# Second-stage units made whole in every chunk of a fused long convolution and gated network on one core

## The chip, the cores and the metric

The kernel runs on one core of one Trainium2 chip. The time is device microseconds from launch to end on that core. The profile names the engines PE (matrix products), PEld (loads of the stationary operand, beside PE), DVE (vector), ACT (scalar functions), POOL (general purpose) and SP, which here only issues transfers. All data are float32; each matrix product of the program shows as two records in the trace, and so does each load of its stationary operand.

## The reference, cut to what matters

```python
x = q = A_q[0]                        # 2048 x 512
g = sigmoid((x * gate_w).sum(-1, keepdims=True))
# branch a
ks = sum(shift(k, ks_ - 1 - j) * shift_k[:, j] for j in range(4))   # causal, 4 taps
kv = ks * v
y = irfft(rfft(kv, 2 * S) * rfft(ssm_k, 2 * S))[:S] + kv * ssm_D    # along the sequence
a = q * y
# branch b
r = x @ w_r
idx = the 2 tokens with the largest r
xs = x[idx]
upd = ((silu(xs @ w_gate) * (xs @ w_up)) @ w_down) * sigmoid(r[idx])
b = x with upd added at rows idx
out = g * a + (1 - g) * b
```

## The kernel before

The 512 channels are worked off in four chunks c of 128. The long convolution is a Fourier transform in two stages written as matrix products, a product in the frequency domain, and two stages back. The steps of a chunk, with the names that stand in the program's order:

- P taps: the four-tap filter as 32x32 matrix products with diagonal matrices, into PSUM; X untap: a DVE transpose of the result into the tile ks; V values: ks times v into the tile kv, on POOL. Chunk 0 does P, X and V in two halves (0a, 0b) over the sequence; chunks 1 to 3 do P and X in one piece.
- A and C: the first stage for the filter and for kv, four batches b each; E and H: the DVE transposes of their results into the tile e. D adds the skip weight into the filter's data, on POOL.
- U: a unit of the second stage into two PSUM banks; G: an ACT copy of one of its two factors (of both, where POOL multiplies); M: the product of the factors into the tile y, on DVE, or on POOL for the units in POOL_PROD. Chunks 1 and 2 have eight whole units w (128 channels each, 16 products of 256 columns). Chunks 0 and 3 (HALF) have eight half units: 64 channels, 32 products of 128 columns, so that I of one half needs four of the eight.
- Q: two POOL passes that sum products in y, so that I needs fewer matrix products; I: the third stage, one for each half hf of the channels, into four banks; F: its transpose on DVE into one of three slots of f; J: the fourth stage, O and K: gate, residual and q; S: the store. In chunk 3 the sums Q are made for half 0 only.

The second branch runs between these: R.0 to R.7 (router and gate), R.cp, R.rr (a transfer into row form), R.mx, R.ix (the two largest, DVE), R.ti, R.xs (gather), then G.g0 to G.u7 (gate and up projections, 16 weight tiles through a ring of four slots wff), G.d0 to G.d7 (down projection, the same ring), G.cp, G.sel, G.upd, and the scatters Z. For the last chunk the residual part goes to a DRAM tile q1 (SQ), Zs adds the update there, and Lq1 brings it back for K.

All of it is recorded in the order of one text, ORDER, which names each step, and behind an @ the PSUM bank or ring slot that it takes. Each engine runs its own steps in that order, and SP issues the loads (Lk, Lh, Lv, Lq, Ls and so on) in it; a step waits for what it reads and for the slot that it writes.

Of the kernel before, what the change touches and what calls it, by code (L numbers as in the profile page):

```python
# [43 lines left out]
M.0.5 Q.0.6 Q.0.4 I.0.0@0 Lk.2@0 X.1 D.2 Q.0.5 F.0.0 R.0@4 R.1 Ls.4@0 R.2 Ls.5@1 D.3 R.3 V.1.1 Ls.6@2 A.1.0@6 Ls.7@3
V.1.2 A.1.2@0 E.1.0 A.1.3@2 V.1.0 E.1.2 C.1.1@6 Lh.4@1 Lv.5@2 V.1.3 A.1.1@0 E.1.3 R.4 Lh.5@0 E.1.1 Lv.6@0 C.1.0@2
Ls.8@0 H.1.1 C.1.2@0 R.5 H.1.0 R.6 Ls.9@1 C.1.3@6 Ls.10@2 H.1.2 R.7 D.4 H.1.3 I.0.1@0 Ls.11@3 R.cp R.rr R.T@5 F.0.1
D.5 U.1.4@6 R.gate U.1.5@4 G.1.4@0 U.1.0@0 M.1.4 G.1.5@1 U.1.1@2 G.1.0@0 M.1.5 U.1.6@6 M.1.0 G.1.1@1 Q.1.2 U.1.7@4
G.1.6@0 M.1.1 J.0.1@0 G.1.7@0 J.0.2@1 O.0.1@0 M.1.7 M.1.6 J.0.0@6 R.mx O.0.2@1 J.0.3@7 U.1.2@4 K.0.1 R.ix P.2@0
G.1.2@1 K.0.2 S.0.1 O.0.0@0 Q.1.0 S.0.2 O.0.3@1 M.1.2 R.ti Lq.1.2@1 U.1.3@4 Lk.3@0 X.2 Lq.1.3@2 K.0.0 A.2.1@6 G.1.3@0
R.xs S.0.0 A.2.3@4 E.2.1 V.2.3 A.2.0@0 E.2.3 A.2.2@2 Lh.6@1 V.2.0 C.2.3@6 E.2.0 Lh.7@0 V.2.2 R.xT@4 Lq.2.0@0 E.2.2  # L50
C.2.0@0 R.xc Lv.7@2 K.0.3 C.2.2@4 H.2.3 G.g0@2 Q.1.3 S.0.3 G.g1 H.2.2 Ls.12@0 G.g2 Ls.13@1 G.g3 R.rs@3 Ls.14@2 H.2.0
P.3@4 Ls.15@3 R.sg D.7 R.fac V.2.1 R.oi Lq.2.1@3 M.1.3 C.2.1@0 X.3 G.g4 D.6 G.g5 Q.1.1 Ls.16@0 G.g6 Ls.17@1 G.g7 H.2.1
Ls.18@2 A.3.3@4 G.sig Ls.19@3 G.m0 A.3.0@6 V.3.3 E.3.3 I.1.1@0 V.3.2 E.3.0 A.3.1@4 V.3.0 F.1.1 A.3.2@6 V.3.1 E.3.1
# [5 lines left out]
C.3.1@0 G.d4 H.3.2 GQ0.1 Lq.3.2@2 G.d5 SQ.0 Q.2.0 C.3.0@6 H.3.1 GQ1.1@1 G.d6 H.3.0 G.d7 GQ0.2 Lq.3.3@1 I.2.0@0 SQ.1
G.cp U.3.0@6 GQ1.2@0 F.2.0 U.3.2@4 G.3.0@0 SQ.2 G.3.2@1 M.3.0 I.2.1@0 GQ1.3@1 M.3.2 Q.3.0 GQ0.3 SQ.3 G.sel@6 F.2.1  # L60
U.3.3@4 Q.3.2 G.upd U.3.1@6 G.3.3@0 M.3.3 U.3.7@0 Z.0 G.3.1@1 U.3.5@2 M.3.1 G.3.7@0 Q.3.3 J.2.0@4 G.3.5@1 M.3.7
U.3.4@6 Q.3.1 O.2.0@0 M.3.5 J.2.3@5 G.3.4@0 K.2.0 I.3.0@0 O.2.3@1 M.3.4 Zs S.2.0 U.3.6@6 F.3.0 K.2.3 J.2.1@4 G.3.6@1
Z.1 S.2.3 J.2.2@5 O.2.1@0 M.3.6 Lq1 J.3.00@0 O.2.2@1 J.3.01@1 K.2.1 O.3.01@0 S.2.1 I.3.1@4 K.2.2 O.3.00@1 S.2.2 K.3.01
# [5 lines left out]
def mixed_kernel(ctx: ExitStack, tc: tile.TileContext, a: dict):  # L69
# [71 lines left out]
    add("Lk.0a", load_k, 0, 0)  # L141
    add("Lk.0b", load_k, 0, 1)
    for c in range(1, NC):
        add(f"Lk.{c}", load_k, c)
# [570 lines left out]
```

## Time and profile before

| | |
|---|---|
| median of three runs | 184.55 us (183.42 to 187.08) |
| profiled execution: time, and span of its instructions | 182.8 us, 181.0 us |
| PE busy | 150.8 us, 3,234 matrix-product records |
| PEld, DVE, POOL, ACT busy | 84.2, 114.5, 94.1, 52.5 us |
| mean granted PE clock | 0.929 |
| moved by DMA | 41.62 MB, 230 GB/s over the span |

The profile is of one execution: the first two lines differ by 1.8 us inside that execution (launch and end), and the median of the runs lies 1.75 us above it. Busy time counts an engine's instructions, so that the span less an engine's busy time is what it stood idle. Lines L... are those of the kernel before.

### The profile page before, as it was taken

To read this page: it belongs to the slowest core of one execution; us is meant where nothing else is said; L and a number is where in the kernel's file an instruction comes from. 1 tells how busy PE (TensorE), PEld (TensorE's weight loads), DVE (VectorE), ACT (ScalarE), POOL (GpSimd) and SP (SyncE) were. 2 spreads that over 40 slices of the span, in tenths; PEclk is the share of its full clock that TensorE was granted. 3 is DMA by queue.
4 is the path that set the end of the run, shared out by engine and by line. 5 is a ranking of instruction groups with operands and counts; after the bars stand their busy time and mean duration, and the time that the engine had idled before them with its cause. 6 is when DMAs were issued, how large, how long until landed. Compare 5 with 4: busy or idle time off the path is not lost.

```text
span 181.0 us, 7115 instructions
## 1 busy us (share of the span) xinstructions
PE 150.8 (83%) x3234; PEld 84.2 (47%) x3234; DVE 114.5 (63%) x90; ACT 52.5 (29%) x123; POOL 94.1 (52%) x94
## 2 busy tenths in 40 slices
PE   7939993497999999999896899999927979799840
PEld 7825353383343366743451234575402346559340
DVE  1025895546489879969799679512970388736462
ACT  3000020222000136851000100499217757467000
POOL 0033406539191006998985820699980026676841
PEclk9996996569999999999999699999985899999997
DMA  5999999900299990068899901999589711016623
GB/s 156 367 380 405 409 412 415 363 21 7 43 352 408 414 369 12 32 173 336 282 364 359 325 30 20 376 252 278 172 263 321 243 66 62 4 62 192 231 106 116
DMA packets 14143, 41.62 MB, mean 230 GB/s; under 512 B 2007, under 2 KB 2336, under 8 KB 13474
## 3 DMA queue, kind: packets, MB, share of 16 engines
q1 hardware_dynamic: 13954, 41.17, 63.9%
q8 instruction: 25, 0.41, 1.0%
q0 software_dynamic: 160, 0.01, 0.1%
q14 instruction: 4, 0.03, 0.0%
HBM read 35.91 MB, written 5.25 MB: 227 GB/s over the span
## 4 chain that ended last, share of the span: by engine, by line
PE 52%; POOL 11%; issue 11%; DMA 10%; DVE 9%; ACT 3%; SPq 1%; POOLq 0%; DVEq 0%
PE ps L287 11%; PE ps L251 8%; PE ps L341 8%; PE ps L244 7%; DMA wff<-in_wg_dram 4%; PE ps L364 4%; DVE f L344 4%; DMA pe<-in_qrow_dram,ti 3%; PE ps L174 3%; POOL y L325 3%; PE ps L194 3%; POOL qN L381 3%; DMA wff<-in_wd_dram 3%; POOL y L326 3%; PE ps L587 2%
## 5 line engine op out<-in xcount | busy, mean ns | idle before, releaser
L237 DVE STREAM_TRANSPOSE e<-ps 128x1024 f32<-128x1024 f32 x32 | 37.9, 1224 | 11.1 <-PE ps L251 8.1
L287 PE MATMUL ps<-e,w 64*32 64x128 f32 (+1 forms) x1536 | 37.7, 330 | 8.5 <-issue 8.5
L314 DVE TENSOR_TENSOR y<-ps,g 128x1024 f32<-128x1024 f32 x28 | 33.3, 1220 | 17.3 <-ACT g L299 17.0
L325 POOL TENSOR_TENSOR y<-y 128x256 f32<-128x256 f32 (+1 forms) x20 | 19.0, 952 | 34.2 <-DVE y L314 34.1
L287 PEld LDWEIGHTS ps<-e,w 64*32 64x32 f32 x1536 | 26.8, 113 | 20.5 <-issue 15.8
L299 ACT ACTIVATE g<-ps 128x512 f32<-128x512 f32 x28 | 16.7, 601 | 48.8 <-PE ps L287 45.9
L215 POOL TENSOR_TENSOR kv<-ks,vN 128x512 f32<-128x512 f32 x16 | 19.9, 1273 | 13.3 <-DVE ks L205 5.8
L344 DVE STREAM_TRANSPOSE f<-ps 128x2048 f32<-128x2048 f32 x8 | 18.5, 2314 | 7.4 <-PE ps L341 7.4
L194 PE MATMUL ps<-kT,diag 32*32 32x512 f32 (+1 forms) x640 | 19.6, 512 | 4.1 <-issue 4.1
L341 PE MATMUL ps<-y,c 32*64 32x512 f32 x288 | 18.7, 615 | 0.5 <-DVE f L344 0.5
L326 POOL TENSOR_TENSOR y<-y 128x256 f32<-128x256 f32 (+1 forms) x20 | 19.0, 951 | 0.0
L244 PE MATMUL ps<-hN,c 64*128 64x512 f32 x64 | 18.8, 721 | 0.2 <-issue 0.2
L377 ACT ACTIVATE o<-ps,omg,gcol 128x128 f32<-128x128 f32 x48 | 17.5, 468 | 3.2 <-PE ps L364 3.2
L364 PE MATMUL ps<-f,vv 128*64 128x128 f32 (+1 forms) x320 | 15.9, 252 | 2.4 <-DVE f L344 2.4
L381 POOL TENSOR_TENSOR qN<-o,qN 128x512 f32<-128x512 f32 x12 | 15.5, 1296 | 4.3 <-ACT o L377 4.0
L251 PE MATMUL ps<-kv,c 64*128 64x512 f32 x64 | 17.4, 655 | 0.0
L364 PEld LDWEIGHTS ps<-f,vv 128*64 128x64 f32 x320 | 14.4, 135 | 5.1 <-DVE f L344 3.4
L194 PEld LDWEIGHTS ps<-kT,diag 32*32 32x32 f32 x640 | 9.9, 103 | 11.3 <-issue 8.5
L314 POOL TENSOR_TENSOR y<-g 128x1024 f32<-128x1024 f32 x4 | 9.6, 2403 | 9.5 <-ACT g L296 9.5
L244 PEld LDWEIGHTS ps<-hN,c 64*128 64x128 f32 x64 | 6.9, 221 | 10.1 <-issue 8.1
L234 POOL TENSOR_TENSOR hN<-hN,drow 65x32 f32<-65x32 f32 x8 | 2.1, 266 | 16.9 <-DMA hN<-in_hN_dram 15.8
L341 PEld LDWEIGHTS ps<-y,c 32*64 32x64 f32 x288 | 6.1, 129 | 9.9 <-issue 7.7
(59 smaller groups left out, 103.9 us busy)
## 6 DMA issues: line engine op xcount, KB each, us to landing
hN<-in_hN_dram SPq DMA_DIRECT2D x8, 512.0 KB, 6.0
vN<-in_vN_dram SPq DMA_DIRECT2D x8, 512.0 KB, 7.1
qN<-in_qN_dram SPq DMA_DIRECT2D x16, 256.0 KB, 6.0
wff<-in_qT_dram SPq DMA_DIRECT2D x8, 512.0 KB, 7.0
wff<-in_wg_dram SPq DMA_DIRECT2D x8, 448.0 KB, 6.7
wff<-in_wu_dram SPq DMA_DIRECT2D x8, 448.0 KB, 4.9
wff<-in_wd_dram SPq DMA_DIRECT2D x8, 448.0 KB, 5.9
kT<-in_kT_dram SPq DMA_DIRECT2D x3, 1120.0 KB, 5.9
```

Source lines behind the costliest of these rows:

```text
L194: nc.tensor.matmul(p[32 * g:32 * g + 32, i, 0:32 * nm], diag[r, 4 * c + j], x, start=(j == 0), stop=(j == 3), skip_group_check=True)
L237: nc.vector.transpose(e[:, place[c, i], b * 16:b * 16 + 16].rearrange("p d k e -> p d e k"), p)
L244: nc.tensor.matmul(p[:, j], w1[r], x[r, 16 * (b % 2):16 * (b % 2) + 16], start=True, stop=True)
L251: nc.tensor.matmul(p[:, par].rearrange("p (d e m) -> p d e m", e=2, m=16), w1[r], x[r], start=True, stop=True)
L287: nc.tensor.matmul(po[32 * j:32 * j + 32, b, ri, :, u], w2[r, k, j, 32 * ri:32 * ri + 32], xs[r, :, :, 8 * j + k, :], start=(ri == 0 and u ...
L314: eng.tensor_mul(z, x.unsqueeze(3).broadcast_to(n).rearrange("p b k h d -> p (b k) h d"), g.unsqueeze(2).broadcast_to(n).rearrange("p b k ...
L325: nc.gpsimd.tensor_tensor(z[:, :, 0, 0], z[:, :, 0, 0], z[:, :, 1, 1], op=ALU.subtract)
L326: nc.gpsimd.tensor_tensor(z[:, :, 0, 1], z[:, :, 0, 1], z[:, :, 1, 0], op=ALU.add)
L341: nc.tensor.matmul(o, w3[r, w], x, start=(n == 0), stop=(n == len(parts) - 1), skip_group_check=True)
L344: nc.vector.transpose(f[:, (2 * c + hf) % 3].rearrange("p d n e -> p d e n"), P["I", c, hf].rearrange("p j (d u) -> p d j u", u=8))
L364: nc.tensor.matmul(p[64 * par:64 * par + 64, i], vv[:, k], x[..., k, :], start=(i == 0), stop=True, skip_group_check=True)
L381: (nc.vector if (c, m) in KDVE else nc.gpsimd).tensor_mul(qn, tiles["o", (c, m)], qn)
```

## The change

Six things are done together:

- Chunks 0 and 3 get whole units, as chunks 1 and 2 have; U, G, M and Q lose their half forms.
- Chunk 0's taps are one run of 64 products of 512 columns behind one load of k; the result goes to two pairs of banks that the order places, and X is two DVE transposes, one for each pair, in every chunk. ks and kv are fixed tiles; gq and q1u (the gate's and the residual's tiles of the last chunk) lie in them. v is laid out on the host so that V reads both operands in a row.
- The sums Q are of whole pairs; in chunk 3 two of the four pairs are summed, and I multiplies the other two unsummed: 16 products of 512 and 16 of 256 columns for each half, where before it were 16 of 512 for half 0 and 32 of 512 for half 1.
- POOL multiplies units 0 and 3 of chunk 0 too (and unit 5 in place of 6 of chunk 2); V.2.0 and V.3.0 move to DVE.
- The start: 4 warm-up products of 512 columns instead of 16 of 128; the step W (an early sigmoid) stands behind the router's gate, so that ACT loads a second function table there.
- ORDER is written anew. `staged` is never called, since STAGE is empty.

```diff
-HALF, LAST = (0, 3), 3
+LAST = 3
-WARM = 16
+WARM = 4
-POOL_PROD = {(1, 3), (1, 6), (2, 3), (2, 6)}
+POOL_PROD = {(0, 0), (0, 3), (1, 3), (1, 6), (2, 3), (2, 5)}
+VDVE = {(2, 0), (3, 0)}
+STAGE = set()
-...(2, 0), (2, 1), (2, 2), (2, 3), (3, 0, 0), (3, 0, 1), (3, 0, 2), (3, 0, 3)}
+...(2, 0), (2, 1), (2, 2), (2, 3), (3, 0), (3, 1)}
 ORDER = """
...
+PW Lc Lk.0@0 Lh.0@0 Ldr Lh.1@1 Lv.0@0 Ls.0@0 DG Lv.1@1 Ls.1@1 Lw2a Ls.2@2 Lc2 Lv.2@2 Lq.0.0@0 P.0@0,2 D.0 D.1 A.0.3@4
...
+    ks = const.tile([128, 4, 512], F32, name="ks")
+    kv = const.tile([128, DC // 2, 16, 2], F32, name="kv")
+    gq = ks.rearrange("p i (m d) -> p (i m) d", d=HC).rearrange("p (h m) d -> p h m d", h=2)
+    q1u = kv.rearrange("p d m e -> p (d m e)").rearrange("p (m d) -> p m d", d=DC)
...
-        z = const.tile([128, 128], F32, name="zero")
+        z = const.tile([128, 512], F32, name="zero")
...
-            nc.tensor.matmul(ps[:, 7, 0:128], z, z, start=True, stop=True)
+            nc.tensor.matmul(ps[:, 7], z[:, 0:128], z, start=True, stop=True)
...
+    def taps(c):
         kt = tiles["kT", c]
+        p = P["P", c] = [ps[:, x:x + 2] for x in at]
         for j in range(4):
             for i in range(4):
                 r = slice(32 * i, 32 * i + 32)
+                x = kt[r, 64 * (3 - j):64 * (3 - j) + 2048].rearrange("p (m z) -> p m z", z=128)
                 for g in range(4):
+                    nc.tensor.matmul(p[i // 2][32 * g:32 * g + 32, i % 2], diag[r, 4 * c + j], x[:, :, 32 * g:32 * g + 32],
                                      start=(j == 0), stop=(j == 3), skip_group_check=True)
...
+    def untap(c, h):
+        nc.vector.transpose(ks[:, 2 * h:2 * h + 2], P["P", c][h])
+
+    def values(c, b):
+        v = tiles["vN", 2 * c + b // 2].rearrange("p (i n) -> p i n", i=2)
+        (nc.vector if (c, b) in VDVE else nc.gpsimd).tensor_mul(
+            kv[:, 16 * b:16 * b + 16].rearrange("p d m e -> p m d e"),
+            ks[:, b].rearrange("p (m d e) -> p m d e", d=16, e=2),
+            v[:, b % 2].rearrange("p (m d e) -> p m d e", d=16, e=2))
...
     def U(c, w):
...
-        if half:
-            xs = xs[:, :, d0 // 2:d0 // 2 + 32]
         pb = P["U", c, w] = bank(2)
+        po = pb.rearrange("p b (r i d) -> p b r i d", r=2, i=2)
+        for ri in range(2):
+            for j in range(4):
+                for b in range(2):
+                    r = slice(64 * b, 64 * b + 64)
+                    nc.tensor.matmul(po[32 * j:32 * j + 32, b, ri], w2[r, w, j, 32 * ri:32 * ri + 32],
+                                     xs[r, :, :, 8 * j + w, :], start=(ri == 0), stop=True, skip_group_check=True)
...
+    def Q(c, v):
+        z = y[:, v].rearrange("p b k h d u -> p b k h (d u)")
```

What the order shows of it, at three places. On PE, from the warm-up to the end of chunk 0's units (`zero` is the warm-up, `kT,diag` P, `hN` A, `kv` C, `e,w` U, `wff,c` R, `y,c` I), before:

```order
L174 MATMUL ps<-zero 128x128 x16
L194 MATMUL ps<-kT,diag 32x256 x128
L244 MATMUL ps<-hN,c_75 128x512 x8
L251 MATMUL ps<-kv,c_75 128x512 x8
L287 MATMUL ps<-e,w_78 32x2x64 x256
L194 MATMUL ps<-kT,diag 32x512 x64
L341 MATMUL ps<-y,c_76 64x512 x16
```

and now:

```order
L174 MATMUL ps<-zero 128x512 x4
L190 MATMUL ps<-kT,diag 32x512 x64
L229 MATMUL ps<-hN,c_75 128x512 x6
L236 MATMUL ps<-kv,c_75 128x512 x2
L229 MATMUL ps<-hN,c_75 128x512 x2
L236 MATMUL ps<-kv,c_75 128x512 x6
L229 MATMUL ps<-hN,c_75 128x512 x4
L264 MATMUL ps<-e,w_78 32x256 x128
L229 MATMUL ps<-hN,c_75 128x512 x2
L415 MATMUL ps<-wff,c_76 32x256 x8
L190 MATMUL ps<-kT,diag 32x512 x64
```

P.0 and the units have half as many products, two batches A of chunk 1 stand ahead of the units, A.2.0 and the first R ahead of P.1, and I.0.0 has gone from behind P.1 to a later place. On DVE in the same stretch (`ks` X, `e` E and H, `y` M, `f` F), before:

```order
L205 STREAM_TRANSPOSE ks<-ps 128x4x8x32 x2
L237 STREAM_TRANSPOSE e<-ps 128x16x2x32 x7
L314 TENSOR_TENSOR y<-ps,g 128x8x2x64 x2
L237 STREAM_TRANSPOSE e<-ps 128x16x2x32
L314 TENSOR_TENSOR y<-ps,g 128x8x2x64 x6
L203 STREAM_TRANSPOSE ks<-ps 128x4x16x32
```

and now:

```order
L194 STREAM_TRANSPOSE ks<-ps 128x1024 x2
L218 STREAM_TRANSPOSE e<-ps 128x16x2x32 x10
L285 TENSOR_TENSOR y<-ps,g 128x1024 x6
L218 STREAM_TRANSPOSE e<-ps 128x16x2x32
L194 STREAM_TRANSPOSE ks<-ps 128x1024 x2
```

All eight exchanges of chunk 0 and two of chunk 1 now stand ahead of the products M, of which two have gone to POOL. On PE at the end (`f,vv` J, `y,c` I, `pe,c` G.sel), before:

```order
L287 MATMUL ps<-e,w_78 32x2x64 x128
L364 MATMUL ps<-f,vv 64x128 x8
L287 MATMUL ps<-e,w_78 32x2x64 x32
L364 MATMUL ps<-f,vv 64x128 x8
L341 MATMUL ps<-y,c_76 64x512 x16
L287 MATMUL ps<-e,w_78 32x2x64 x32
L364 MATMUL ps<-f,vv 64x128 x16
L364 MATMUL ps<-f,vv 64x64 x32
L341 MATMUL ps<-y,c_76 64x512 x32
L364 MATMUL ps<-f,vv 64x64 x32
```

and now (`wff,hT` is G.d):

```order
L264 MATMUL ps<-e,w_78 32x256 x32
L553 MATMUL ps<-wff,hT 32x256 x16
L333 MATMUL ps<-f,vv 64x128 x16
L568 MATMUL ps<-pe_1620,c_76 2x512
L310 MATMUL ps<-y,c_76 64x512 x16
L310 MATMUL ps<-y,c_76 64x64x4 x16
L310 MATMUL ps<-y,c_76 64x512 x16
L310 MATMUL ps<-y,c_76 64x64x4 x16
L333 MATMUL ps<-f,vv 64x64 x64
```

The first I of the last chunk stood ahead of its last unit; now both stand behind all units, behind the down projection and behind G.sel. The four steps O of the last chunk stand on DVE behind both F, two of which stood ahead of the last F before; O.3.01 and O.3.11 take the slots of the ring o that O.3.00 and O.3.10 took.

## Rows read from the trace of the kernel before

**Rows 1.** Page, part 1: busy time, share of the span, records.
```profile
PE 150.8 (83%) x3234; PEld 84.2 (47%) x3234; DVE 114.5 (63%) x90; ACT 52.5 (29%) x123; POOL 94.1 (52%) x94
```
**Rows 2.** PE in order of time: start, us, what, count [idle before it].
```profile
6.70 4.00 PE L194 MATMUL ps<-kT,diag 32*32 32x256 f32 x191
13.65 1.50 PE L194 MATMUL ps<-kT,diag 32*32 32x256 f32 x65 [2.95 <-issue]
...
23.99 2.80 PE L287 MATMUL ps<-e,w 64*32 64x128 f32 x155
29.93 3.66 PE L287 MATMUL ps<-e,w 64*32 64x128 f32 x128 [3.15 <-issue]
35.98 3.48 PE L287 MATMUL ps<-e,w 64*32 64x128 f32 x128 [2.39 <-issue]
...
43.63 4.02 PE L194 MATMUL ps<-kT,diag 32*32 32x512 f32 x102 [1.13 <-issue]
```
**Rows 3.** DMA queues of the page: packets, MB, share.
```profile
q8 instruction: 25, 0.41, 1.0%
```
**Rows 4.** Stretches: length, busy (records) by engine, granted PE clock, DMA share, GB/s.
```profile
29.93:33.60 3.67, 3.66 (x128) 3.21 (x127) 1.23 (x1) 1.01 (x2) 0.30 (x2) 0.50 1.02 414
39.71:42.50 2.79, 2.79 (x127) 1.68 (x128) 2.49 (x3) 1.32 (x3) 2.52 (x4) 1.00 0.02 6
81.15:175.94 94.79, 81.05 (x1650) 42.29 (x1650) 61.85 (x48) 35.10 (x87) 58.27 (x50) 0.95 0.63 208
```
**Rows 5.** Who waited for whom, PE: us in total, times, longest.
```profile
PE ps L587 <- DMA wff<-in_wd_dram: 4.4, 2, 4.0
```
**Rows 6.** PE in order of time, 50 to 80 us: R, A, I, U, J, P.
```profile
50.12 1.93 PE L449 MATMUL ps<-wff,c 128*32 128x256 f32 x32 [0.49 <-DVE ks L203]
51.99 2.85 PE L244 MATMUL ps<-hN,c 64*128 64x512 f32 x12
...
61.88 2.07 PE L341 MATMUL ps<-y,c 32*64 32x512 f32 x32
...
65.06 5.96 PE L287 MATMUL ps<-e,w 64*32 64x256 f32 x192
70.95 3.75 PE L364 MATMUL ps<-f,vv 128*64 128x128 f32 x64
...
75.65 4.46 PE L194 MATMUL ps<-kT,diag 32*32 32x512 f32 x128
```
**Rows 7.** Groups by line and shape: busy us, mean ns | idle before.
```profile
L237 DVE STREAM_TRANSPOSE e<-ps 128x1024 f32<-128x1024 f32 x32 | 37.9, 1224 | 11.1 <-PE ps L251 8.1 <-PE ps L244 2.8
L314 DVE TENSOR_TENSOR y<-ps,g 128x1024 f32<-128x1024 f32 x28 | 33.3, 1220 | 17.3 <-ACT g L299 17.0
...
L325 POOL TENSOR_TENSOR y<-y 128x512 f32<-128x512 f32 x8 | 10.3, 1291 | 6.2 <-DVE y L314 6.0
...
L314 POOL TENSOR_TENSOR y<-g 128x1024 f32<-128x1024 f32 x4 | 9.6, 2403 | 9.5 <-ACT g L296 9.5
...
L167 ACT ACT_TABLE_LOAD x1 | 1.3, 1283 | 0.7 <-PEq L701 0.7
```
**Rows 8.** A stretch, products U alone: length, PE, PEld busy, granted clock, DMA.
```profile
144.20:165.90 21.70, 9.72 (x512) 7.70 (x512) 1.00 0.20 60
```
**Rows 9.** All engines at the end, DVE rows: the last F, O and K.
```profile
171.48 2.32 DVE L344 STREAM_TRANSPOSE f<-ps 128x2048 f32<-128x2048 f32 x1 [1.84 <-PE ps L341]
...
176.05 0.69 DVE L423 TENSOR_TENSOR o<-ps,ks 128x512 f32<-128x512 f32 x1 [0.24 <-PE ps L364]
176.78 0.93 DVE L428 TENSOR_TENSOR o<-o,kv 128x512 f32<-128x512 f32 x1
```
**Rows 10.** DMA issues: engine, count, KB each, us from issue to landing.
```profile
kv<-q SPq DMA_DIRECT2D x1, 1024.0 KB, 5.6
out_dram<-o SPq DMA_DIRECT2D x4, 256.0 KB, 2.0
...
q<-pe,oidx POOLq DMA_INDIRECT x1, 2.6
```

More of the change, by code (lines that the diff above doesn't have):

```diff
@@ L44 @@
[L44 to L53, printed above, removed]
@@ L59 @@
[L59 to L63, printed above, removed]
@@ new lines @@
+S.1.3 I.2.1@4 Ls.24@0 SQ.0 GQ1.1@1 U.3.0@2 F.2.1 GQ0.1 G.u5 G.u6 G.u7 R.sg Lq.3.2@4 G.3.0@0 Ls.25@1 U.3.1@4 M.3.0
+Ls.26@2 U.3.2@6 Ls.27@3 SQ.1 U.3.6@2 G.m1 Lq.3.3@3 G.3.2@1 R.fac G.3.1@0 M.3.2 G.T@0 J.2.2@1 G.hT M.3.1 GQ1.2@0 G.d0@0
+G.d1 Ls.28@0 G.d2 G.3.6@1 SQ.2 G.d3 Ls.29@1 M.3.6 O.2.2@1 U.3.7@6 Ls.30@2 Ls.31@3 U.3.4@4 G.3.7@0 K.2.2 J.2.0@1
+G.3.4@1 M.3.7 U.3.3@2 Q.3.0 S.2.2 O.2.0@0 U.3.5@6 G.3.3@0 G.d4 GQ1.3@1 G.d5 M.3.3 K.2.0 G.d6 G.d7 M.3.4 J.2.3@1 SQ.3
+G.cp Q.3.1 G.3.5@0 J.2.1@0 O.2.3@0 M.3.5 G.sel@2 I.3.0@4 G.upd O.2.1@1 Zs K.2.3 GQ0.3 I.3.1@0 F.3.0 K.2.1 GQ0.2 Lq1
@@ L140, in mixed_kernel @@
     add("Lvv", load, vv, a["vv"])
[L141 to L144, printed above, removed]
+    for c in range(NC):
+        add(f"Lk.{c}", lambda c: load(slot("kT", c), a["kT"][c]), c)
     for t in range(2 * NC):
@@ L226, in mixed_kernel @@
+    for c in range(NC):
         add(f"P.{c}", taps, c)
-        add(f"X.{c}", untap, c)
+        for h in range(2):
+            add(f"X.{c}{'ab'[h]}", untap, c, h)
         for b in range(4):
@@ L234, in skip, with exchange, staged @@
         nc.gpsimd.tensor_add(x[0:65, :, 0], x[0:65, :, 0], drow[:, t])
-    def exchange(c, i, b, p):
-        nc.vector.transpose(e[:, place[c, i], b * 16:b * 16 + 16].rearrange("p d k e -> p d e k"), p)
+    def exchange(k, c, b):
+        p = tiles.get((k, c, b)) if (k, c, b) in STAGE else P["AC"[k == "H"], c, b]
+        x = p.rearrange("p j (d n) -> p (j d) n", n=N2) if k == "E" else p.rearrange("p a (d m) -> p d a m", m=16)
+        nc.vector.transpose(e[:, place[c, k == "H"], b * 16:b * 16 + 16].rearrange("p d k e -> p d e k"), x)
+    def staged(k, c, b):
+        t = tiles[k, c, b] = slots["g2"][:, at[0]].rearrange("p (j n) -> p j n", j=2)
+        nc.scalar.activation(t, P["AC"[k == "H"], c, b], AF.Copy)
     def A(c, b):
@@ L301, in M @@
     def M(c, w):
-        half, v, ks, d0 = unit(c, w)
         fi, vi = order(c)[2]
@@ L329, in I @@
         p = P["I", c, hf] = bank(4)
-        runs = [(0, 4)], [(v, v + 1) for v in range(4) if not summed(c, hf, v)]
+        runs = [(0, 4)], [(v, v + 1) for v in range(4) if not summed(c, v)]
         if len(runs[1]) > 1 and runs[1][-1][1] - runs[1][0][0] == len(runs[1]):
@@ L350, in mixed_kernel @@
                 add(f"{fn.__name__}.{c}.{w}", fn, c, w)
-        for w in range(8 if c in HALF else 4):
-            if summed(c, w // 4, w % 4):
-                add(f"Q.{c}.{w}", Q, c, w)
+        for v in range(4):
+            if summed(c, v):
+                add(f"Q.{c}.{v}", Q, c, v)
         for hf in range(2):
@@ L412, in back @@
     def back():
-        t = tiles["q1u",] = small([128, 16, DC], "kv")
-        load(t, q1)
+        load(q1u, q1)
     add("Lq1", back)
```

128 lines of the change are left out of this document (37 added, 91 removed).

## The prediction, on record before the run

> **What bounds the kernel now.** I first set PE's busy time against the span: 150.8 of 181.0 us [rows 1]. No other engine is near it, so the question is where PE stands for the other 30 us and why. In order of time [rows 2] PE stops at 10.70 for 2.95 us, at 26.78 for 3.15, at 33.60 for 2.39 and at 42.50 for 1.13: 9.6 us before chunk 0 is done. The reader should see where the stops lie: after 191 records of P.0, after 155 records of the units, then each 128 records, inside a step and not at its start, so no operand is awaited. One queue carries "instruction" packets [rows 3]: 25 of 0.41 MB, 16 KB each, for 3,234 product records and as many weight loads, that is 259 instructions or some 128 product records a packet. From restart to restart it is 6.05 us (29.93 to 35.98), most of that with the DMA engines at 1.02, and 3.9 us (39.71 to 43.63) with them at 0.02 [rows 2, 4]. I read the stops as PE out of its own instructions, and 6.05 and 3.9 us as the least time of a packet with the DMA engines full and idle. In the same place the granted clock is 0.50, the lower level of 1.2 GHz, and 64 records of a half unit take 1.83 us (3.66 for 128). Behind 81.15 PE is busy 81.05 of 94.79 us up to the last J [rows 4]; the largest single wait there is 4.4 us for the down projection's weights [rows 5].
>
> The Trainium skill, page "Runtime: NRT & Kernel Launch", section "Instruction fetch mechanics", says that instructions come in blocks of 256 and that fetching the next one is mostly hidden. The block agrees with rows 3; rows 2 have 9.6 us that are not hidden. By that page the stops would have another cause and could stay, and the sum below would come out some 8 us higher; that time is the first rival's.
>
> **The change, part by part.** Durations at the full clock [rows 6]: A or C 0.95 to 1.0 (2.85 for three), R 0.48, I 2.05, a whole unit 0.99 (5.96 for six), J 0.94, P 4.46. On the others [rows 7]: exchange E or H 1.22, M 1.22 on DVE, 2.40 on POOL, one pass of Q on a whole pair 1.29.
>
> *Up to the first unit.* P.0 starts when the warm-up ended before, 6.7, or up to 0.5 later, because its load is now one piece; take 6.8. In one run it takes 4.46, not the 8.45 from 6.70 to 15.15, and ends at 11.2. From there DVE has two X and eight exchanges in a row, 10 x 1.22 = 12.2, under which the A and C lie. The units start at 23.5; before, 23.99. So P.0's 4 us are not gained here; DVE takes them for exchanges that the first half units did not need, and A.1.1 and A.1.0 are done under them.
>
> *To the end of P.1.* DVE: two exchanges of chunk 1 and six M, 8 x 1.22 = 9.8, and some 0.7 of hand-overs, to 34.0; the units (8 x 0.99) lie under it. They are 256 records, two packets instead of four; by the intervals above one wait of up to 1.5 is left, while loads still run. Take 1.3 on DVE's line: 35.3, P.1 to 39.8. Before, it ended at 47.65 [rows 2]: 7.8 us ahead. POOL has two M and three Q here, 2 x 2.40 + 6 x 1.29 = 12.5, from 26.8 to 39.4, just before X.1 frees V.1; that is covered by nothing, a microsecond later there is one later for all. R.z and the new places of ks and kv cost nothing while DVE is the line. Of the loads, Lk.1 stands on SP behind Lh.4, which waits for A.1.0, at 23 to 24; the 2.7 MB from there at the 414 GB/s of rows 4 are 6.5 us, so k lands by 31 and is wanted at 35.
>
> *To the last unit of chunk 1.* PE is the line: six R 2.9, three A and four C 7.0, two I 4.1, P.2 4.46, eight units 7.95, hand-overs 0.3: 26.7, to 66.5. Before, this point is 81.15, with R.T and J.0 done as well (1.2 and 3.75) and A.2.0 and A.2.1 not (1.9): 3.1 us of work, so the gain is 11.5.
>
> *To the last J.* Before, PE is busy 81.05 from 81.15 on [rows 4]. Add 3.1; take off what chunk 3's units lose, 9.72 [rows 8] less 8 x 0.99, 1.8: 82.4. I of chunk 3 has the same columns (48 products of 512 before, 32 and 32 halves now). Idle then: 13.7 us before, of which three instruction waits in chunk 3 and the one for F.3.1 go or shrink. I take 1.4 for named hand-overs (the gate's bank, the gather, F.3.1). The load waits I bound by 0 (the G steps are now in pieces of one to four with other work between) and 7 (about what all loads cost before); nearer to the lower end, 2.5. So 66.5 + 82.4 + 1.4 + 2.5 = 152.8. V.2.0 and V.3.0 on DVE cost 0.69 to 0.93 each [rows 9], and X in halves 0.2 a chunk; DVE has room under PE here, except R.fac and G.m1 ahead of chunk 3's M. The second table costs ACT 1.28 [rows 7] while A.2.3 waits for the gate's bank, 0.5 of it on PE, in the 1.4.
>
> The Trainium skill, page "ScalarE: Activation LUTs", section "What ACT_TABLE_LOAD costs", adds a drain of 1.38 us to each change of table. The 1,283 ns agree with rows 7, no row shows a drain; by the page the sum would be 1.4 us more.
>
> *The end.* Before, from F's start at 171.48 to its end 173.80, and 7.2 us more to 181.0. Now behind the last F: O 0.69; a wait for Lq1, because G.sel stands directly ahead of I.3.0: update 0.7, scatter 1.3 and 2.6, load 5.6 [rows 10] end 10.6 after I.3.0 starts, against 9.2 for two I of 3.1, F and O, so 1.4; two K on POOL 2.5; the store's landing 2.2, because O.3.01 and O.3.11 need the ring slots of O.3.00 and O.3.10; O 0.69, K 0.93, and 3.3 from that K's end (177.71) to 181.0 as before. Together 11.7, 4.5 more than before. The last J ends 2.1 after F, so 9.6 follow it: 162.4.
>
> **The sum.** Span 162.4, against its own 181.0; with 1.8 of launch 164.2 against 182.8; and the median of the runs lies 1.75 above that execution: **166 us**, 10% faster.
>
> **The rivals.**
>
> *The stops stay.* If PE stops by the traffic and not by the number of its instructions, P.0 and the units keep three stops, 8.3 us, of which 1.3 is in the sum: +7.0; and if the clock is then 0.50 again, whole units take up to 1.98, +8 for chunk 0 less what lies under DVE's 9.8. 173 to 179. For it: rows 4 show the longest stop under full DMA, and the loads of the first 30 us are as many as before. Against: rows 2 and 4 have a stop of 1.13 with the DMA engines idle, and no step of fewer records per microsecond has one.
>
> *The second branch becomes the line.* From its first product with the gathered rows (86.9) to its last G.d (142.3) it took 55 us before; the gather's result now comes at 90, and J.2.3, J.2.1, G.sel, both I, F and the end, 3 + 6.2 + 2.5 + 11.7 = 23.4, stand behind it in PE's order. If it keeps its pace the span is 90 + 55.4 + 23.4 = 168.8, and the median 172. It decides as soon as the branch takes more than about 49 us. For it: rows 5, and SP now has stores between the weight loads. Against: the waits for weights are what made it 55.
>
> *The end eats it: slower.* Both I of chunk 3 now stand behind its last M (3.1 that lay under other work), and the end is 4.5 longer: 7.6 us. This makes the kernel slower than before by over 2% if all else gains less than 3.9; with no gain at all 192. Only stops that all stay, with the slow clock, could bring that about.
>
> **How the numbers follow.** Forecast 0.66 (160 to 171); stops stay 0.14; second branch 0.13; slower 0.04; no change that a measurement here can tell (within 2%) 0.03. With the waits for loads and packets and the hand-overs of the last two parts at nothing, and A and C at 0.95, the sum is 160, and one less is the spread of the durations: 159. The upper end takes in the second branch and most of the first rival: 178. Faster by over 2%: 0.91; within 2%: 0.05, with the top of the first rival; slower by over 2%: 0.04.
>
> **What would show it.** Right: P.0 one piece of about 4.5 us; units of chunk 0 from 23 to 24 at the full clock and at most one stop in them; P.1 over before 41; last unit of chunk 1 before 69; the last F some 11 to 12 us ahead of the end. Wrong: stops of 2 to 3 us in P.0 or in the units; PE waiting for V.1 behind POOL's sums; waits for weights above 5 us between 90 and 140; DVE with M of chunk 3 late behind R.fac.

## The result, and the profile after

| | before | changed kernel |
|---|---|---|
| median, on the same chip | 183.99 us (180.94 to 187.08, 4 runs) | 169.28 us (168.27 to 174.25, 4 runs) |
| ratio | | 0.930, 95% interval 0.914 to 0.945 |
| matrix-product records | 3,234 | 2,602 |

The kernel is 7% faster; the forecast was 166 us, 10% faster. Some executions of every kernel run some per cent longer at a lower granted clock, among them the profiled one of the changed kernel (174.25 us, span 172.5, its others 168.27 to 170.58): the ratio, and every median of the experiments, leave such executions out, and a later profiled execution of the same kernel, the control of the last experiments (170.15 us, span 168.4), stands beside it where a length matters.

The page of the changed kernel, part 1, the instruction queue of part 3, and PE's granted clock in 40 slices of part 2:

```profile
PE 143.4 (83%) x2602; PEld 73.2 (42%) x2602; DVE 111.1 (64%) x93; ACT 53.8 (31%) x124; POOL 95.2 (55%) x82
...
PEclk9999969999999999999999999999969999999975
...
q8 instruction: 20, 0.33, 0.8%
```

Against [rows 1, 3]: 632 product records fewer and five packets fewer, and again 5,204 records by 20 packets, 260 a packet. PE's busy time fell by 7.4 us and the span by 8.5 (12.6 in the control), so the rest came out of waits. PE in order of time, changed kernel (start, us, shape, records, idle before):

```profile
7.25 4.47 PE L190 MATMUL ps<-kT,diag 32*32 32x512 f32 x128
...
22.70 3.61 PE L229 MATMUL ps<-hN,c 64*128 64x512 f32 x8 [2.61 <-POOL hN L213]
...
26.24 5.00 PE L264 MATMUL ps<-e,w 64*32 64x256 f32 x172
32.88 2.80 PE L264 MATMUL ps<-e,w 64*32 64x256 f32 x84 [1.64 <-issue]
...
38.00 5.08 PE L190 MATMUL ps<-kT,diag 32*32 32x512 f32 x128
...
64.72 5.45 PE L264 MATMUL ps<-e,w 64*32 64x256 f32 x192 [0.32 <-ACT g L272]
```

The reader should see P.0 in one piece where [rows 2] has a stop of 2.95, and the units in two pieces with one stop of 1.64 where [rows 2] has 3.15 and 2.39, and at the full clock (granted 1.00 from 26.24 to 35.68). P.1 ends at 43.08, before at 47.65; the last unit of chunk 1 ends at 70.17. The same places in the control, PE:

```profile
22.18 1.99 PE L229 MATMUL ps<-hN,c 64*128 64x512 f32 x8 [1.51 <-POOL hN L213]
24.09 4.99 PE L264 MATMUL ps<-e,w 64*32 64x256 f32 x172
29.72 2.80 PE L264 MATMUL ps<-e,w 64*32 64x256 f32 x84 [0.64 <-issue]
```

What PE waited for over the span, in the first profiled execution again (us in total, times, longest):

```profile
PE ps L516 <- DMA wff<-in_wu_dram: 3.9, 1, 3.9
PE ps L264 <- issue: 3.4, 2, 1.7
...
PE ps L516 <- DMA wff<-in_wg_dram: 2.4, 2, 1.7
...
PE ps L553 <- DMA wff<-in_wd_dram: 0.5, 1, 0.5
```

The waits for weights, 6.8 us together, are the largest item left. In the control they are spread and as long:

```profile
PE ps L553 <- DMA wff<-in_wd_dram: 2.6, 3, 1.1
PE ps L516 <- DMA wff<-in_wu_dram: 2.6, 4, 0.8
PE ps L516 <- DMA wff<-in_wg_dram: 1.8, 2, 1.0
```

The end of the control, DVE, POOL and SP in order of time (the other half of [rows 9]):

```profile
153.27 2.32 DVE L313 STREAM_TRANSPOSE f<-ps 128x2048 f32<-128x2048 f32 x1 [0.43 <-PE ps L310]
...
157.53 2.47 POOL L394 TENSOR_TENSOR o<-o,kv 128x512 f32<-128x512 f32 x2 [1.91 <-DMA kv<-q]
158.82 6.55 SPq L397 DMA_DIRECT2D out_dram<-o  x4
161.59 1.29 DVE L389 TENSOR_TENSOR o<-ps,ks 128x512 f32<-128x512 f32 x2 [4.00 <-DMA out_dram<-o]
...
162.75 1.70 POOL L394 TENSOR_TENSOR o<-o,kv 128x512 f32<-128x512 f32 x1
162.91 2.10 DVE L394 TENSOR_TENSOR o<-o,kv 128x512 f32<-128x512 f32 x1
```

From the last F's end, 155.59, to the span's end it is 12.8 us: first the load of q1 (POOL waits for `kv<-q`), then DVE stands 4.00 us until a store has freed the slot of o, then K.3.11 takes 2.10 us beside a POOL pass.

### The profile page after: what moved, and what is told of

The parts are those of the page before. It is cut to its first block, busy times and chain, and to the rows that moved or that the text cites. A ratio compares the mean times of both kernels' runs of the same rounds, so it can differ in the third digit from the quotient of the medians.

```text
span 172.5 us, 5847 instructions
## 1 busy us (share of the span) xinstructions
PE 143.4 (83%) x2602; PEld 73.2 (42%) x2602; DVE 111.1 (64%) x93; ACT 53.8 (31%) x124; POOL 95.2 (55%) x82
## 4 chain that ended last, share of the span: by engine, by line
PE 45%; DMA 24%; issue 11%; POOL 7%; DVE 6%; ACT 5%; POOLq 0%; ACTq 0%; DVEq 0%; SPq 0%
PE ps L190 9%; PE ps L264 9%; PE ps L229 8%; PE ps L236 5%; DMA wff<-in_wu_dram 5%; DMA hN<-in_hN_dram 4%; PE ps L310 4%; DMA q<-o 4%; DMA kv<-q 4%; PE ps L174 3%; DMA wff<-in_wg_dram 3%; PE ps L415 3%; PE ps L333 2%; DMA out_dram<-o 2%; DMA q<-pe,oidx 1%
## 5 line engine op out<-in xcount | busy, mean ns | idle before, releaser
L218 DVE STREAM_TRANSPOSE e<-ps 128x1024 f32<-128x1024 f32 x32 | 37.7, 1223 | 10.4 <-PE ps L229 6.6
L285 DVE TENSOR_TENSOR y<-ps,g 128x1024 f32<-128x1024 f32 x26 | 31.2, 1229 | 15.5 <-ACT g L275 14.8
L264 PE MATMUL ps<-e,w 64*32 64x256 f32 x1024 | 32.1, 377 | 4.1 <-issue 3.4
L264 PEld LDWEIGHTS ps<-e,w 64*32 64x32 f32 x1024 | 19.4, 104 | 18.7 <-issue 7.7
L198 POOL TENSOR_TENSOR kv<-ks,vN 128x512 f32<-128x512 f32 x14 | 17.7, 1292 | 8.2 <-DVE ks L194 8.2
L310 PE MATMUL ps<-y,c 32*64 32x512 f32 (+1 forms) x320 | 19.4, 603 | 0.1
L294 POOL TENSOR_TENSOR y<-y 128x512 f32<-128x512 f32 x14 | 18.7, 1338 | 0.1
L190 PE MATMUL ps<-kT,diag 32*32 32x512 f32 x512 | 18.5, 597 | 0.0
L295 POOL TENSOR_TENSOR y<-y 128x512 f32<-128x512 f32 x14 | 18.0, 1282 | 0.0
L285 POOL TENSOR_TENSOR y<-g 128x1024 f32<-128x1024 f32 x6 | 14.5, 2412 | 5.8 <-ACT g L272 5.8
L194 DVE STREAM_TRANSPOSE ks<-ps 128x1024 f32<-128x1024 f32 x8 | 9.5, 1223 | 12.3 <-PE ps L190 11.4
L516 PE MATMUL ps<-wff,xsT 128*32 128x224 f32 x128 | 7.9, 364 | 6.3 <-DMA wff<-in_wu_dram 3.9
```

The source lines that it names most:

```text
L190: nc.tensor.matmul(p[i // 2][32 * g:32 * g + 32, i % 2], diag[r, 4 * c + j], x[:, :, 32 * g:32 * g + 32], start=(j == 0), stop=(j == 3), s ...
L198: (nc.vector if (c, b) in VDVE else nc.gpsimd).tensor_mul(kv[:, 16 * b:16 * b + 16].rearrange("p d m e -> p m d e"), ks[:, b].rearrange("p ...
L218: nc.vector.transpose(e[:, place[c, k == "H"], b * 16:b * 16 + 16].rearrange("p d k e -> p d e k"), x)
L264: nc.tensor.matmul(po[32 * j:32 * j + 32, b, ri], w2[r, w, j, 32 * ri:32 * ri + 32], xs[r, :, :, 8 * j + w, :], start=(ri == 0), stop=True ...
L285: eng.tensor_mul(y[:, w // 2, :, :, :, :, w % 2].rearrange("p b k h d -> p (b k h) d"), x.unsqueeze(3).broadcast_to(n).rearrange("p b k h ...
L294: nc.gpsimd.tensor_tensor(z[:, :, 0, 0], z[:, :, 0, 0], z[:, :, 1, 1], op=ALU.subtract)
```

## The experiments

The theory: PE's stops come from the number of its own records, and what is left after the change is the loads of the second branch and the end. The rival on the front half: the stops come from the traffic on the DMA engines. The rival on the middle: the place of the loads in SP's queue, not their bytes. Kernels of one group ran on one chip.

### Group 1: do the records make the stops?

The kernel before had 179.27 us here (one run).

**The changed kernel again**, with no edit.

> The changed kernel as it is, for a profile of an undisturbed execution and as the measure for the three beside it. All theories: 168 to 171 us, PE with one stop of 1 to 2 us in the units of chunk 0 and one in those of chunk 3, and some 6 us of waits for the weights of the second branch.

Measured: 171.5 us (four runs, 170.47 to 172.74); its trace is of an execution of 177.06 us.

**Chunk 0's units in products of 128 columns.** Twice the records for the same columns, at the same places; nothing else:

```diff
+SPLIT = (0,)
-                    nc.tensor.matmul(po[32 * j:32 * j + 32, b, ri], w2[r, w, j, 32 * ri:32 * ri + 32],
-                                     xs[r, :, :, 8 * j + w, :], start=(ri == 0), stop=True, skip_group_check=True)
+                    for h in range(2 if c in SPLIT else 1):
+                        d = slice(32 * h, 32 * h + 32) if c in SPLIT else slice(0, 64)
+                        nc.tensor.matmul(po[32 * j:32 * j + 32, b, ri, :, 2 * d.start:2 * d.stop],
+                                         w2[r, w, j, 32 * ri:32 * ri + 32], xs[r, :, d, 8 * j + w, :],
+                                         start=(ri == 0 and h == 0), stop=True, skip_group_check=True)
```

> Order, loads and sums of the changed kernel; each product of chunk 0's units is two of 128 columns, so that these units are 512 records again where they are 256, with the same columns. If PE stops because it runs out of instructions (theory), the units take two packets more, at 3.9 to 6.05 us each for what takes 2 us of PE time: the last unit of chunk 0 ends 5 to 9 us later than the 35.7 of the changed kernel, and the total is 4 to 8 us longer. If the new order and the new loads made the gain and the stops come from the traffic alone (rival), the same columns at the same clock cost nothing: within 1 us.

Measured: 177.75 us (two runs), 6.3 more; 22 packets. PE in order of time:

```profile
26.25 4.36 PE L267 MATMUL ps<-e,w 64*32 64x128 f32 x172
31.62 2.76 PE L267 MATMUL ps<-e,w 64*32 64x128 f32 x128 [1.01 <-issue]
37.54 6.14 PE L267 MATMUL ps<-e,w 64*32 64x128 f32 x212 [3.16 <-issue]
```

The same loads, the same start, and a stop of 3.16 is back, 128 records behind the one before. The units end at 43.7, in the unedited kernel of this group at 36.2.

**The same edit in chunk 1** (`SPLIT = (1,)`), where the DMA engines are about half busy.

> The same doubling in chunk 1, whose units run while the DMA engines have little to do (62 to 70 us). Theory: a packet needs 3.9 us with idle DMA engines too, so 512 records take 15 to 16 us where 256 took 7.8, with stops of 1 to 2 us every 128 records: total 5 to 8 us longer. Rival (stops are made by the traffic): no stop here, within 1 us.

Measured: 179.1 us (two runs, 177.75 and 180.42), 7.6 more; 22 packets. PE in order of time, in an execution of 182.08 us:

```profile
61.18 5.40 PE L267 MATMUL ps<-e,w 64*32 64x128 f32 x263
67.82 2.71 PE L267 MATMUL ps<-e,w 64*32 64x128 f32 x128 [1.24 <-issue]
73.19 4.00 PE L267 MATMUL ps<-e,w 64*32 64x128 f32 x121 [2.66 <-issue]
```

Stops now stand in a step that had none, with a DMA share of 0.54. Traffic alone does not make them.

**As many records as before, in the new order**: chunk 0's taps in halves of 256 columns and the units of chunks 0 and 3 split.

```diff
+SPLIT = (0, 3)
-                        nc.tensor.matmul(p[i // 2][32 * g:32 * g + 32, i % 2], diag[r, 4 * c + j], x[:, :, 32 * g:32 * g + 32],
+                    for m in ((slice(0, 8), slice(8, 16)) if c == 0 else (slice(0, 16),)):
+                        nc.tensor.matmul(p[i // 2][32 * g:32 * g + 32, i % 2, 32 * m.start:32 * m.stop],
+                                         diag[r, 4 * c + j], x[:, m, 32 * g:32 * g + 32],
```

> Chunk 0's taps and the units of chunks 0 and 3 in twice as many products with the same columns: as many instructions as before the change, in the order, with the loads and the sums of after it. Theory: some five packets more, 10 to 15 us, 179 to 184 us: the gain is nearly all gone. Rival (the order made the gain): 170 to 173 us.

Measured: 184.88 us (one run), 13 more than the changed kernel and 5.6 more than the one run of the kernel before; 25 packets. The waits for "issue" of the units alone (L269) and of P (L192), in an execution of 189.51 us:

```profile
PE ps L269 <- issue: 8.2, 6, 3.1
PE ps L192 <- issue: 2.0, 1, 2.0
```

By these runs the new order without the smaller number of records is worth nothing; it is slower than before. So the gain needs the fewer records. That they make all of it is not shown: with fewer records the order may count too.

The runs together size a packet. From restart to restart, that is from the end of one stop to the end of the next, with 128 records between, against the DMA share of that stretch (length, busy of PE, PEld, DVE, ACT, POOL with records, granted clock, DMA share, GB/s; the first of the split of chunk 0, the second of that of chunk 1, the others of the last kernel):

```profile
31.62:37.54 5.92, 2.76 (x128) 2.48 (x128) 2.45 (x2) 1.21 (x2) 4.55 (x4) 1.00 0.88 358
```

```profile
67.82:73.19 5.37, 2.71 (x128) 2.48 (x128) 2.65 (x3) 1.62 (x2) 2.75 (x2) 1.00 0.54 185
```

```profile
39.36:44.46 5.10, 3.83 (x128) 3.35 (x129) 2.45 (x2) 1.19 (x2) 2.37 (x2) 0.67 0.55 221
44.46:48.19 3.73, 2.75 (x129) 2.48 (x129) 1.06 (x1) 1.09 (x2) 0.13 (x1) 1.00 0.02 4
```

With the kernel before this is 6.05 us at a share of 0.96 (29.93 to 35.98; the 1.02 of [rows 4] is of its first 3.67), 5.92 at 0.88, 5.1 to 5.4 at 0.55, 3.7 to 3.9 at 0.02. Chunk 3 has more such stretches, which widen it: 3.45 at 0.02 in the kernel before (155.49 to 158.94), 4.27 at 0.34 and 5.65 at 1.02 in this one, and 7.55 at 0.97 in the last experiment (128.79 to 136.34). The rival is right in this much: traffic goes with a longer packet, and the share alone does not fix the length. A packet can stop PE only where 128 records last less than it takes: they last 2.8 us at 128 columns, 3.7 at 256 (4.99 for 172), 4.46 at 512.

### Group 2: single parts, and the two terms that came out too small

The kernel before had 179.15 us here. The changed kernel itself was not run on this chip: of the edits to it the traces are read, and what they are worth in total is not shown here.

**Whole units and sums in chunk 0 alone, in the kernel before**: chunk 0 leaves HALF, its SUMS become whole pairs, and its H, U and Q move in ORDER as that needs.

```diff
-HALF, LAST = (0, 3), 3
+HALF, LAST = (3,), 3
-C.0.3@0 E.0.2 U.0.3@2 H.0.3 U.0.0@6 G.0.3@0 G.0.0@1 U.0.2@0 M.0.3 M.0.0 U.0.1@2 G.0.2@0 Q.0.3 H.0.2 G.0.1@1 Q.0.0
+C.0.3@0 E.0.2 H.0.3 H.0.2 U.0.3@2 U.0.0@6 G.0.3@0 G.0.0@1 U.0.2@0 M.0.3 M.0.0 U.0.1@2 G.0.2@0 G.0.1@1 M.0.2 Q.0.1
```

> The kernel before with one part of the change alone: chunk 0's units and sums whole. Its old order is kept; only the last exchanges of chunk 0 stand ahead of the units and the sums behind their pairs. Theory (instructions): two packets fewer in chunk 0, the units start 2 to 3 us later and end at 36 to 38 instead of 41.4, P.1 3 to 5 us earlier, total 178 to 181 against some 183.5. Rival (order): within 1 us of the kernel before, since none of the new order is there.

Measured: 176.7 us (two runs), 2.5 less. PE in order of time, and its largest waits:

```profile
25.90 9.24 PE L287 MATMUL ps<-e,w 64*32 64x256 f32 x256 [3.17 <-DVE e L237]
```

```profile
PE ps L587 <- DMA wff<-in_wd_dram: 5.9, 4, 2.9
PE ps L194 <- issue: 4.0, 2, 2.9
```

The units run without a stop, though at a granted clock of 0.82, at which 128 records last 4.6 us; the stop of 1.06 is in P.1 (38.07). P.1 ends at 41.9, 5.7 earlier than in the trace of before. That trace is of another chip, with a span of 181.0 against 175.7 here, so between these two executions 5.3 reach the end; the medians on one chip say 2.5, and how much of the 5.7 is the edit's stays open.

**The first small weights later in SP's queue.** Units started at 26.24 and not at 23.5 because PE waited 2.61 us for POOL's skip weight D.2, which waited for the load of h, issued at 14.59 and landed some 7.6 us later, with the Ls loads issued ahead of it. Those four go behind Lk.1:

```diff
-PW Lc Lk.0@0 Lh.0@0 Ldr Lh.1@1 Lv.0@0 Ls.0@0 DG Lv.1@1 Ls.1@1 Lw2a Ls.2@2 Lc2
+PW Lc Lk.0@0 Lh.0@0 Ldr Lh.1@1 Lv.0@0 DG Lv.1@1 Lw2a Lc2
...
+G.0.6@0 Lk.1@0 Ls.0@0 Ls.1@1 Ls.2@2 Ls.3@3
```

> The changed kernel with the first three router loads (1.5 MB) moved on SP from the start to behind the load of k for chunk 1. In its trace A.1 waits 2.6 us for D.2, which waits for the load Lh.2. If that wait is what made the units of chunk 0 start at 26.2 and not at 23.5 as predicted, they start 2 to 3 us earlier here and the total is 1 to 2.5 us shorter. If DVE or the instruction packets hold the units anyway (rival), the total stays within 0.7 us.

Measured: 168.98 us; ratio to before 0.943 (0.937 to 0.950). PE in order of time, in an execution of 172.54 us:

```profile
23.52 4.99 PE L264 MATMUL ps<-e,w 64*32 64x256 f32 x172 [1.13 <-DVE e L218]
30.94 2.80 PE L264 MATMUL ps<-e,w 64*32 64x256 f32 x84 [2.42 <-issue]
```

The units start at 23.52, as forecast, and the stop then is 2.42 instead of 1.64. They end at 33.7, 2 us ahead of 35.7 and not 2.7; the control, which started at 24.09 with a stop of 0.64, ended them sooner still, at 32.5. Against the control an earlier start gains nothing: the packet came later than there.

**Stores out of the way of the weight loads.** S.1.1 goes behind Ls.15, and Ls.18 ahead of Lq.2.3, on SP:

```diff
-Q.2.0 E.3.3 S.1.1 Ls.14@2 U.2.6@2 Ls.15@3 G.2.5@0
+Q.2.0 E.3.3 Ls.14@2 U.2.6@2 Ls.15@3 S.1.1 G.2.5@0
```

> The changed kernel with two moves on SP: the store S.1.1 behind the weight load Ls.15, and the weight load Ls.18 ahead of the two q loads that wait for stores. PE waits there 6.3 us for gate and up weights. If those waits are loads held up on SP behind stores (theory), 2 to 4 us of them go and the total is 1 to 3 us shorter. If the weights' landing is set by what the DMA engines carry (rival), the waits stay and the total is within 0.7 us.

Measured: 171.96 us; ratio to before 0.957 (0.949 to 0.965). The waits for weights are 3.9, 2.2 and 0.7, 6.8 as in the changed kernel. The place of these loads in the queue is not what makes them.

**The end without the wait for a slot of o.** O.3.01 and O.3.11 write into a tile that is free by then, and the scatter Z.2 goes behind K.3.01:

```diff
-        t = slot("o", (LAST, n)).rearrange("p (i d) -> p i d", i=8)
+        if m == 0:
+            t = slot("o", (LAST, n))
+        else:
+            t = tiles["o", (LAST, n)] = slots["g2"][:, 0, 512 * hf:512 * hf + 512]
+        t = t.rearrange("p (i d) -> p i d", i=8)
```

> The changed kernel with O.3.01 and O.3.11 written into the free slot of g2 instead of the ring o, and the last scatter Z.2 behind K.3.01 on POOL. At the end DVE waits 3.7 us for a store's landing. Theory: from the last F to the end 12.5 us become about 10, the total is 2 to 2.5 us shorter. Rival: K on POOL and the landing of Lq1 are the line anyway, and less than 0.7 us goes.

Measured: 169.13 us; ratio to before 0.947 (0.938 to 0.957). The end in order of time:

```profile
154.25 2.32 DVE L313 STREAM_TRANSPOSE f<-ps 128x2048 f32<-128x2048 f32 x1 [0.43 <-PE ps L310]
...
158.47 2.48 POOL L398 TENSOR_TENSOR o<-o,kv 128x512 f32<-128x512 f32 x2 [1.83 <-DMA kv<-q]
158.50 1.28 DVE L393 TENSOR_TENSOR g<-ps,ks 128x512 f32<-128x512 f32 x2
...
159.81 1.69 DVE L398 TENSOR_TENSOR g<-g,kv 128x512 f32<-128x512 f32 x1
160.91 1.70 POOL L398 TENSOR_TENSOR g<-g,kv 128x512 f32<-128x512 f32 x1
```

From the last F's end, 156.57, to the span's end, 167.1, it is 10.5 us instead of 12.8. What stands there now is the load of q1, 1.83 on POOL.

### Group 3: what the loads are worth

The kernel before had 181.2 us here.

**The control**, the changed kernel with no edit.

> The changed kernel once more, as the measure for the kernels beside it: 168 to 172 us; from the last F to the end some 12 us, waits for weights 6 to 8 us in all.

Measured: 171.4 us (five runs); ratio to before 0.944 (0.937 to 0.951).

**The edits that helped, together**: the two of group 2 on the first loads and on the end, and W back ahead of the warm-up, so that no function table is loaded in the middle.

```diff
-PW Lc Lk.0@0 Lh.0@0 Ldr
+W PW Lc Lk.0@0 Lh.0@0 Ldr
```

> The changed kernel with three moves together: the end's products in the slot of g2 with Z.2 behind K.3.01, the first router loads behind the load of k for chunk 1, and the step W back at the start, so that ACT loads one function table. Theory (the end's wait and the load of the filter are on the line): the end 2.5 to 3 us shorter, the units of chunk 0 some 2.5 us earlier of which the packet stop takes one back, W at most 0.4: 165 to 167 us, 3 to 5 less than the control. Rival (each only moves the wait to another place): within 1 us of the control.

Measured: 169.0 us (five runs), 2.3 less than the control, where 3 to 5 were expected; ratio to before 0.934 (0.928 to 0.941). The last F's end to the span's end is 10.3, 2.5 less; the units start at 23.19, 0.9 ahead of the control, again stop for 2.42 and end at 33.4, 0.9 behind it; the waits for weights are 7.5. It is the best version that was run, and what it gains is about the end's.

**Half of the bytes of the second branch's weights.** Each of the 24 tiles is loaded only in the first half of its columns; the rest of it holds what was there, so that the update of the two chosen rows is not the reference's. All products stay.

```diff
-        load(t[:side[n].shape[0], :side[n].shape[1]], side[n])
+        k = side[n].shape[1] // (2 if n >= 8 else 1)
+        load(t[:side[n].shape[0], :k], side[n][:, :k])
```

> The changed kernel with only the first half of the columns of each of the 24 weight tiles of the second branch loaded (5.4 MB less), all products kept; the second branch's update is not the reference's. If the 6 to 8 us that PE waits for weights is the time that their bytes take behind other loads (theory now), at most 1.5 us of it is left and the total is 3 to 6 us shorter. If it is the order of issue, each load waiting for its ring slot and for the steps ahead of it on SP (rival), the waits stay above 4 us and the total is within 2 us.

Measured: 161.0 us, 10.4 less than the control, where 3 to 6 were expected; ratio to before 0.886 (0.879 to 0.893). The waits for weights go from 7.0 to 0.4. One step in the middle, here and (second fence) in the control, PE:

```profile
129.19 1.97 PE L265 MATMUL ps<-e,w 64*32 64x256 f32 x64
```

```profile
136.25 3.29 PE L264 MATMUL ps<-e,w 64*32 64x256 f32 x64
```

From the last unit of chunk 1 to the last J it is 80.9 us (68.23 to 149.13) instead of 90.0 (67.68 to 157.7): 9.1 less, 6.6 of it the waits themselves and 1.3 this step, which in the control ran at a granted clock of 0.57 behind them. From 91 to 145 us the control's DMA engines are nearly full:

```profile
91.00:145.00 54.00, 46.49 (x852) 23.91 (x854) 31.09 (x31) 25.80 (x67) 29.67 (x23) 0.97 0.90 279
```

**Chunk 3's units in products of 128 columns** (`SPLIT = (3,)`).

> The doubling of the products in chunk 3's units alone. The prediction put these units at 1.8 us of busy time and the instruction waits among them at 2.7. Theory: 256 records more are two packets; other steps of few records lie between these units, so 2 to 5 us longer than the control. Rival (no packet is short there): within 1 us.

Measured: 176.1 us, 4.7 more than the control; ratio to before 0.967 (0.958 to 0.976); 22 packets. PE stops for 0.66 and 1.04 in the units, and for 2.50 inside G.d, whose records stand between the units':

```profile
128.79 2.01 PE L267 MATMUL ps<-e,w 64*32 64x128 f32 x85 [0.66 <-issue]
...
136.34 1.07 PE L558 MATMUL ps<-wff,hT 112*32 112x256 f32 x10 [2.50 <-issue]
...
145.71 0.71 PE L267 MATMUL ps<-e,w 64*32 64x128 f32 x26 [1.04 <-issue]
```

## Why the prediction was right, and where it was off

**The mechanism held.** Fewer records, fewer packets, and the stops go. Splitting the units again brings the stops back at the packet's interval in three places (+6.3, +7.6, +4.7), and with all records of before the new order is slower than before. The first rival, stops by the traffic, falls as a cause of its own and stays as what goes with a packet's length (the three stops that it counts sum to 8.5 and not 8.3). The least time of a packet, read as 3.9, is 3.45 in another stretch of the trace before. The Trainium skill's rule that the prediction weighed is that fetching the next block is mostly hidden ("Runtime: NRT & Kernel Launch", "Instruction fetch mechanics"). These runs agree with it in the taps of 512 columns of the changed kernel, which show no stop; at 128 columns 1 to 3 us a packet were not hidden.

**Step by step**, forecast against the control and, in brackets, the first profiled execution:

| | forecast | measured |
|---|---|---|
| P.0 starts | 6.8 | 7.83 (7.25) |
| units of chunk 0 start | 23.5 | 24.09 (26.24) |
| stop in them | 1.3 | 0.64 (1.64) |
| P.1 ends | 39.8 | 40.15 (43.08) |
| last unit of chunk 1 ends | 66.5 | 67.7 (70.2) |
| from there to the last J's end | 86.3 | 90.0 (91.9) |
| waits for weights in it | 2.5 | 7.0 (6.8) |
| last F's end to the end | 11.7 | 12.8 (12.5) |
| span | 162.4 | 168.4 (172.5) |

The span of the control is 6.0 above the sum: 1.2 up to chunk 1's last unit, 3.7 in the middle, 1.1 at the end.

**The mis-sized term** is the loads' waits in the middle. I bounded them by 0 and 7 and took 2.5 because the G steps are in smaller pieces; they measured 7.0. Moving two loads and a store in the queue did not change them; halving the bytes removed all but 0.4. From 91 to 145 us of the control the DMA share is 0.90: pieces of G spread over the same bytes wait as long in sum. PE's busy time from the last unit of chunk 1 to the last J was 81.08, 1.3 less than the 82.4 of the sum, and this paid a part back. V.2.0 and V.3.0 on DVE, put at 0.69 to 0.93, took 1.37 and 1.43 there.

**The second rival** therefore came true. PE's first product with the gathered rows and its last G.d in the control:

```profile
90.97 0.41 PE L486 MATMUL ps<-c,pe 2*128 2x2 f32 x4 [0.32 <-ACT g L272]
...
142.70 1.93 PE L553 MATMUL ps<-wff,hT 112*32 112x256 f32 x32
```

The branch took 53.7 us (90.97 to 144.63), near the 55.4 before and above the 49 from which the rival was to decide, and 23.8 stood behind it. The rival's sum was 90 + 55.4 + 23.4 = 168.8, the control's span is 168.4, the forecast's 162.4; 4.7 of the 6.0 between the last two are the 53.7 against 49. With half of the bytes the branch took 44.5 (91.52 to 136.06), below the 49, and the span was 159.7. The rival's 172 us are near the control's median of 171.4, the forecast's 166 is not; on the chip of the first comparison the median was 169.28, between the two. So the front half went as the forecast has it and the middle as its rival: that the time still lies in the range is owed to a range wide enough for both.

**The units' start** was 0.6 to 2.7 late for a reason that the sum did not have: D.2 behind a load of h. Lk.1 was the load of the front half that the sum followed; the h tile of chunk 1, which the earlier A.1.1 wants sooner, was not. A part of the 2.7 is the clock: behind the stop of 2.61 the two A of chunk 1, which stand ahead of the units, ran at a granted clock of 0.53, most of it the lower level of 1.2 GHz, and took 3.61; in the control, behind a stop of 1.51, they ran at 1.00 and took 1.99. (Granted clocks of 22.70 to 26.30 and of 22.18 to 24.17; the rows are in the section on the result.)

Moving the loads put the start where the sum has it, 2.7 ahead of the first execution; 0.8 of that went into the packet's stop, and against the control nothing was left.

**The end** was priced with the right pieces. The wait for the slot of o is there (4.00 on DVE, counted from O.3.10), and removing it gives back 2.3. The wait for Lq1 was added up wrongly, from terms that give 10.2 and not 10.6; it took 10.1 from I.3.0's start (147.43 to 157.53). What the sum lacked is that K.3.11 takes 2.10 and not the 0.93 of [rows 9], since it now starts almost with a POOL product (last section).

**The signs.** Of those named for "right", the control shows P.0 in one piece, one stop in the units, P.1 over before 41 and the last unit of chunk 1 before 69; its units start at 24.09 and its last F ends 12.8 ahead of the end, both just outside, and the first execution is late in P.1 and the last unit (43.08 and 70.2). Of those named for "wrong", there is no stop in P.0, PE waits 0.4 for V in the whole span, and M of chunk 3 is not behind R.fac (0.15 us there); waits for weights above 5 us did show, and they are the part in which the forecast was wrong. The slower rival did not come about. The second table cost PE 0.4 us: ACT loaded it in 1.28 (68.76 in the control), and its next instruction began 0.02 behind the load.

**What stays open**: why the load of h held PE 0.5 us longer in the first profiled execution than in the control, which with the lower clock behind it (1.6) makes the 2.2 us between the two starts of the units; and by how much each other part of the change (POOL's share of M, the sums in chunk 3, V on DVE) counts, which no run here separates. Whole units of chunk 0 alone, in the old order, gave 2.5, where the whole change gives 9.8 on the control's chip.

## What to carry to other kernels

Count the records of an engine's program, not only its columns: where PE's products are so short that a packet's worth of them (here 128 product records with their weight loads) runs in less than a packet takes to arrive (3.5 to 3.9 us with idle DMA engines, 5.7 to 7.6 with full ones), wider products pay beyond their busy time, and an earlier start can go into the stop (0.9 earlier, 1.8 more of stop, in the best version against the control). When the front of a kernel gets faster, look for the stretch with the highest DMA share behind it and take the waits for its bytes from before unchanged, however the steps that use them are cut up. And test such a cause in reverse: splitting the products again at one place costs one run.
